# Down products of the experts with w2 stationary and rows moving, in halves of the rows, and the last expert done half by half

## The chip, the cores and the metric

The kernel runs on one core of a Trainium2 chip. The metric is the device time in microseconds (us) of one execution. The engines are named as the profile names them: PE (TensorE, the matmuls) with PEld (its weight loads), DVE (VectorE), ACT (ScalarE), POOL (GpSimd) and SP (SyncE, which issues most DMAs).

## The reference

A linear attention feeds a mixture of experts, which feeds a gated layer. What matters here is the middle part and the handing on to the last:

```python
for e in range(E):                       # 8 experts, x is 3072 x 384, F = 1024
    for k in range(2):                   # each token goes to its top 2 experts
        mask = top2[:, k] == e
        if not mask.any():
            continue
        h = np.maximum(x[mask] @ w1[e], 0.0)
        out[mask] += top2_w[mask, k, None] * (h @ w2[e])
...
a = x @ w_a                              # 384 x 1536 each
b = x @ w_b
return (a * b @ w_out).astype(np.float32)
```

## The kernel before

All is fp32, and every product is made of three matmuls on operands split in two (`prod3`: high by high, high by low, low by high; lines 799, 800 and 801 of the profile).

**Rows of an expert.** An expert gets about 768 of the tokens. Its rows are laid out for 832 (`CAP`); 768 of them (`MAIN`) are always computed, the last 64 only where the routing gave the expert more than 768. `more_rows[e]` is a register of PE, loaded from the tile `tails` (`load_more_rows`), and `tc.If` branches on it. In the profiled data experts 1, 2 and 7 have more than 768 rows and experts 0 and 3 to 6 have not: on line 835, in the other branch of `up_tail`, ten matmuls stand, two for each of five experts.

**Up phase** (`up_unit`). For each of 8 slices `f` of the hidden layer, w1 is stationary (128x128) and the rows X move, 384 columns at a time, twice: 9 matmuls for each, 144 for an expert. ACT writes the rectified high part H to `HB` (line 816), DVE the low part (line 817). Banks 2 to 5 of PSUM take turns.

**Tail and down phase.** `up_tail` does the last 64 rows the other way round (rows stationary, w1 moving, 18 matmuls of 512 columns), then 8 PE transposes bring them into `HB`. `down_unit(e, j)` takes 128 rows at a time: H is stationary and w2 moves (24 matmuls of 384 columns). ACT copies the bank out (`o`, line 890) and SP writes 128 rows to the DRAM tensor `y2` in one DMA (line 891). `down_tail` does the same for the last rows, or one filler matmul. Banks 6 and 7 take turns, so a unit can start when the unit two before it has been copied out.

**What runs beside it.** While expert e is computed, the rows of expert e+1 are gathered (POOL, line 478), transposed in blocks of 32 by DVE (`x_blocks`, line 506), written to the DRAM tensor `xt` and read back in pieces of 384 bytes (`x_out`, `x_in`: SP, lines 514 and 521), and split into X (`x_part`: ACT line 528, DVE line 529). That may not begin before X is free, so it stands in the down phase: `x_part(e+1, j)` goes ahead of `down_unit(e, j)` in the program. Weights come in chunks (`w_load` on SP, `w_split` on ACT and POOL), four chunks ahead. `bg` advances a decoding of the last layer's weights (DVE lines 953 to 963, POOL 960 and 961). Each engine works through its own instructions in the order in which the program wrote them.

**Handing on to the last layer.** For a block of 512 tokens `gather2` fetches both expert rows of each token from `y2` (POOL, line 986), `x2_sum` adds them, and the result is turned into the layout X2. For the first block this is done by PE transposes (`x2_unit`, line 486) inside the last unit of expert 7. The first block may only use the first 256 rows of expert 7 (`CAPL`, `early`), so `gather2` waits for the first two units of expert 7 alone. Later blocks go through DVE and `xt`, as the rows of the experts do. The last layer (`up2_unit`, `down2_unit`) starts when X2 is there; its chunks of weights lie in free parts of W, X, HB and in `EX` (7 slots).

Of the kernel before, what the change touches and what calls it, by code (L numbers as in the profile page):

```python
# [21 lines left out]
DM = H * D  # L22
# [9 lines left out]
CAPL = 256  # L32
CAP = 832
MAIN = 768
# [22 lines left out]
def moe_kernel(ctx: ExitStack, tc, qka, afirst, v, wgn, noise, w1, w2, w3, out):  # L57
# [736 lines left out]
    outs = sctx.enter_context(tc.tile_pool(name="outs", bufs=4))  # L794

    def prod3(ps, a, b, first, last):

        (ah, al), (bh, bl) = a, b
        nc.tensor.matmul(ps, ah, bh, start=first, stop=False)  # L799
        nc.tensor.matmul(ps, ah, bl, start=False, stop=False)  # L800
        nc.tensor.matmul(ps, al, bh, start=False, stop=last)  # L801

    upn = [0]

    def up_unit(e, f, cols):

        for s0, n in cols:
            s = slice(s0, s0 + n)
            pu = bank(2 + upn[0] % 4)[:, :n]
            upn[0] += 1  # L810
            for k in range(KD):
                ks = slice(k * 128, k * 128 + 128)
                prod3(pu, (w1h(f)[:, ks], w1l(f)[:, ks]), (Xh[:, k, s], Xl[:, k, s]), k == 0, k == KD - 1)
                if k == 1:
                    tick()
            nc.scalar.activation(Hh[:, f, s], pu, AF.Relu)  # L816
            nc.vector.scalar_tensor_tensor(Hl[:, f, s], pu, 0.0, Hh[:, f, s].bitcast(F32),  # L817
                                           op0=ALU.max, op1=ALU.subtract)
            tick()

    def up_tail(e):

        s = slice(CAP - 128, CAP)
        n = CAP - MAIN
        w = [W[:, i * 3072:i * 3072 + 3072].rearrange("p (f k n) -> p k f n", f=NF1, k=KD) for i in range(2)]
        pu = [bank(2 + (upn[0] + i) % 4) for i in range(2)]
        upn[0] += 2
        with tc.If(more_rows[e] > 0) as c:
            for i in range(2):
                f = slice(4 * i, 4 * i + 4)  # L830
                for k in range(KD):
                    prod3(pu[i], (Xh[:, k, s], Xl[:, k, s]), (w[0][:, k, f], w[1][:, k, f]), k == 0, k == KD - 1)
        with c.Else():
            for i in range(2):
                nc.tensor.matmul(pu[i], Xh[:, 0, s], w[0][:, 0, 4 * i:4 * i + 4], start=True, stop=True)
        hr = []
        if e < E - 1:
            t = tl(dec, [128, 2, 512], F32, "hr")
            for i in range(2):
                nc.scalar.activation(t[:, i], pu[i], AF.Relu)  # L840
                hr += [t[:, i, q * 128:q * 128 + 128] for q in range(4)]
        else:
            for q, m in ((0, 3), (3, 3), (6, 2)):
                t = tl(rows, [128, DM], F32, "row")
                for i in range(2):
                    a, b = max(q, 4 * i), min(q + m, 4 * i + 4)
                    if a < b:
                        nc.scalar.activation(t[:, (a - q) * 128:(b - q) * 128],
                                             pu[i][:, (a - 4 * i) * 128:(b - 4 * i) * 128], AF.Relu)
                hr += [t[:, c * 128:c * 128 + 128] for c in range(m)]  # L850
        yield
        pt = trbank()
        r = slice(128 - n, 128)
        with tc.If(more_rows[e] > 0) as c:
            for f in range(NF1):
                nc.tensor.transpose(pt[:, f * n:f * n + n], hr[f][r], ident[r, r])
        with c.Else():
            nc.tensor.matmul(pt[:, :NF1 * n], w2h(0)[:, :128], HB[:, :NF1 * n], start=True, stop=True)
        pt = pt[:, :NF1 * n].rearrange("p (f n) -> p f n", f=NF1)
        s = slice(MAIN, CAP)  # L860
        nc.scalar.activation(Hh[:, :, s], pt, AF.Copy)
        nc.vector.tensor_tensor(Hl[:, :, s], pt, Hh[:, :, s].bitcast(F32), op=ALU.subtract)
        yield

    def down_tail(e):
        s = slice(CAP - 128, CAP)
        pd = bank(6 + MAIN // 128 % 2)[:, :DM]
        with tc.If(more_rows[e] > 0) as c:
            for f in range(NF1):
                prod3(pd, (Hh[:, f, s], Hl[:, f, s]), (w2h(f), w2l(f)), f == 0, f == NF1 - 1)  # L870
        with c.Else():
            nc.tensor.matmul(pd, Hh[:, 0, s], w2h(0), start=True, stop=True)
        o = tl(outs, [128, DM], F32, "o")
        r0 = MAIN - (CAP - 128)
        nc.scalar.activation(o[r0:], pd[r0:], AF.Copy)
        nc.sync.dma_start(y2[base_of(e) + MAIN:base_of(e) + CAP], o[r0:])

    def down_unit(e, j, mid={}):
        c0 = min(128 * j, CAP - 128)
        s = slice(c0, c0 + 128)  # L880
        pd = bank(6 + j % 2)[:, :DM]
        for f in range(NF1):
            prod3(pd, (Hh[:, f, s], Hl[:, f, s]), (w2h(f), w2l(f)), f == 0, f == NF1 - 1)
            if f % 2:
                tick()
            if f in mid:
                mid[f]()
        o = tl(outs, [128, DM], F32, "o")
        r0 = 128 * j - c0
        nc.scalar.activation(o[r0:], pd[r0:], AF.Copy)  # L890
        nc.sync.dma_start(y2[base_of(e) + 128 * j:base_of(e) + c0 + 128], o[r0:])


    NEX = 7

    def w3_slot(n):
# [12 lines left out]
        c = 2 * KD * BLK + 6 * BLK + (n - 8) * 768  # L909
# [11 lines left out]
    def p_part(u):  # L921
        c = 2 * KD * BLK + 2 * BLK * (u % 3)
        return HB[:, c:c + BLK], HB[:, c + BLK:c + 2 * BLK]
# [93 lines left out]
    NA = CAPA // 128  # L1017
    for f in range(NF1):
        up_unit(0, f, [(0, CAPA)])
    small.clear()  # L1020
    for j in range(NA):
        down_unit(0, j, {f: (lambda q=q: x_unit(0, q)) for f, q in ((1, 3), (3, 4), (5, 5))} if j == NA - 1 else {})
    for f in range(NF1):
        if f == 1:
            x_unit(0, NJ - 1)
        up_unit(0, f, [(CAPA, MAIN - CAPA)])
        if f == 2:
            load_more_rows(0)
        if f >= NF1 - 4:
            w_load()  # L1030
        tick()
        bg()
# [4 lines left out]
    tail = up_tail(0)  # L1037
    next(tail)
    for n in range(3):
        down_unit(0, NA + n, {f: (lambda q=q: x_unit(1, q))  # L1040
                              for f, q in ((), ((0, 0), (3, 1), (6, 2)), ((0, 3), (2, 4), (4, 5), (6, 6)))[n]})
        next(tail, 0)
        for _ in range((3, 3, 2)[n]):
            w_split()
            w_load()
        bg()
    down_tail(0)

    for e in range(1, E - 1):
        for f in range(NF1):  # L1050
            up_unit(e, f, [(0, MAIN // 2), (MAIN // 2, MAIN // 2)])
            if f == 2:
# [14 lines left out]
        tail = up_tail(e)  # L1067
# [226 lines left out]
```

## Time and profile before

| | us |
|---|---|
| median of 3 executions (lowest, highest) | 1064.31 (1063.27, 1064.66) |
| the profiled execution | 1065.93 |
| its span, from the first to the last instruction | 1064.2 |
| PE busy in it | 1028.1 (97%) |
| DVE, ACT, POOL busy | 518.3, 417.9, 410.9 |
| mean granted TensorE clock, as a share of 2.4 GHz | 0.982 |

The span has three stages: attention with routing up to about 153 us, the experts up to about 608 us, the last layer to the end. The profile's matmul ends are modelled, and one matmul's record reaches into the next, so this document reads distances between the starts of matmuls, not their lengths. A row of the timeline has the start, the length, the engine, the line, the operation, output and inputs, and in brackets the idle time before it with what ended it.

### The profile page before, as it was taken

How to read it: one execution, taken by the hardware profiler on the slowest of the kernel's cores; microseconds unless marked ns; L12 is line 12 of the kernel's file. 1: busy time of each engine (PE TensorE's matmuls, PEld its weight loads, DVE VectorE, ACT ScalarE, POOL GpSimd, SP SyncE). 2: the span in 40 equal slices, each digit the busy share in tenths (PEclk: the TensorE clock that was granted, in tenths of full speed). 3: DMA queues.
4: the chain of work that ended last, by engine and by line, in shares of the span. 5: the costliest groups of instructions: out<-in, count | busy, mean ns of one | idle time of the engine just before them, and what ended most of it. 6: DMA issues, size and time to landing. Idle time of an engine off the chain costs nothing.

```text
span 1064.2 us, 17897 instructions
## 1 busy us (share of the span) xinstructions
PE 1028.1 (97%) x6868; PEld 950.8 (89%) x6868; DVE 518.3 (49%) x940; ACT 417.9 (39%) x913; POOL 410.9 (39%) x446
## 2 busy tenths in 40 slices
PE   8999689999999999999999899999999999999997
PEld 6988679999999999999999788888888888888886
DVE  7999666564554656575652445233242233332221
ACT  2455332564544555555554334322222222222212
POOL 4688432583755666666663443220020020000000
PEclk9999779999999999999999899999999999999999
DMA  7877111567575777686752534213022030020000
GB/s 275 289 284 270 53 54 51 183 211 203 178 214 173 214 226 217 202 241 211 236 171 80 186 89 126 90 45 75 30 76 44 30 109 11 30 60 1 30 1 32
DMA packets 98749, 141.04 MB, mean 133 GB/s; under 512 B 39520, under 2 KB 82656, under 8 KB 98656
## 3 DMA queue, kind: packets, MB, share of 16 engines
q1 hardware_dynamic: 92128, 120.13, 36.5%
q0 software_dynamic: 6528, 19.67, 6.0%
q8 instruction: 58, 0.95, 0.4%
q14 instruction: 35, 0.29, 0.1%
HBM read 101.43 MB, written 38.34 MB: 131 GB/s over the span
## 4 chain that ended last, share of the span: by engine, by line
PE 79%; DVE 6%; DMA 3%; POOL 2%; issue 2%; ACT 1%; SPq 0%; POOLq 0%; ACTq 0%; DVEq 0%
PE bank L799 25%; PE bank L800 25%; PE bank L801 25%; DMA raw<-xt 2%; DVE pm L655 1%; DMA xt<-tb 1%; DVE D L620 1%; DVE A L624 1%; PE bank L650 1%; PE bank L666 1%; PE bank L486 1%; SPq L521 0%; POOL row L986 0%; POOL row L478 0%; POOL W L110 0%
## 5 line engine op out<-in xcount | busy, mean ns | idle before, releaser
L110 POOL TENSOR_TENSOR W<-wst,W 128x384 fp32r<-128x384 f32 x136 | 140.3, 1037 | 138.7 <-ACT W L109 137.1
L799 PE MATMUL bank<-W,HB 128*128 128x384 f32 x528 | 179.9, 341 | 1.6 <-ACT o L890 1.6
L801 PE MATMUL bank<-W,HB 128*128 128x384 f32 x528 | 177.8, 337 | 0.0
L800 PE MATMUL bank<-W,HB 128*128 128x384 f32 x528 | 177.6, 336 | 0.0
L1127 DVE TENSOR_TENSOR p<-bank,a 128x512 f32<-128x512 f32 x72 | 49.8, 691 | 256.6 <-PE bank L801 252.4
L799 PE MATMUL bank<-X,W 128*128 128x384 f32 (+1 forms) x483 | 168.7, 349 | 0.8 <-DVE HB L817 0.8
L800 PE MATMUL bank<-X,W 128*128 128x384 f32 (+1 forms) x483 | 168.1, 348 | 0.0
L801 PE MATMUL bank<-X,W 128*128 128x384 f32 (+1 forms) x483 | 167.9, 348 | 0.0
L986 POOL DMA_INDIRECT row<-y,row x48 | 47.0, 979 | 187.7 <-DVE row L994 170.4
L1125 ACT ACTIVATE a<-bank 128x512 f32<-128x512 f32 x72 | 43.0, 597 | 165.6 <-PE bank L801 163.6
L1129 ACT ACTIVATE HB<-p 128x512 fp32r<-128x512 f32 x72 | 45.5, 632 | 157.3 <-DVE p L1127 150.4
L799 PEld LDWEIGHTS bank<-W,HB 128*128 128x128 f32 x528 | 100.0, 189 | 4.3 <-ACT o L890 2.6
L800 PEld LDWEIGHTS bank<-W,HB 128*128 128x128 f32 x528 | 99.9, 189 | 1.7
L801 PEld LDWEIGHTS bank<-W,HB 128*128 128x128 f32 x528 | 99.7, 189 | 0.0
L799 PEld LDWEIGHTS bank<-X,W 128*128 128x128 f32 x483 | 91.4, 189 | 5.0 <-DVE HB L817 1.3
L801 PEld LDWEIGHTS bank<-X,W 128*128 128x128 f32 x483 | 91.4, 189 | 3.9
L800 PEld LDWEIGHTS bank<-X,W 128*128 128x128 f32 x483 | 91.4, 189 | 3.9 <-issue 0.3
L817 DVE SCALAR_TENSOR_TENSOR HB<-bank,HB 128x384 fp32r<-128x384 f32 x128 | 68.7, 552 | 53.3 <-ACT HB L816 45.1
L816 ACT ACTIVATE HB<-bank 128x384 fp32r<-128x384 f32 x128 | 62.0, 490 | 81.1 <-PE bank L801 75.0
L478 POOL DMA_INDIRECT row<-xd,idx x56 | 59.4, 1061 | 40.0 <-DVE idx L387 23.1
L1130 DVE TENSOR_TENSOR HB<-p,HB 128x512 fp32r<-128x512 f32 x72 | 49.8, 692 | 50.2 <-ACT HB L1129 49.5
L109 ACT ACTIVATE W<-wst 128x384 fp32r<-128x384 f32 x144 | 73.0, 520 | 3.2 <-issue 2.1
(262 smaller groups left out, 1962.8 us busy)
## 6 DMA issues: line engine op xcount, KB each, us to landing
wst<-w SPq DMA_DIRECT2D x128, 192.0 KB
ring<-qka SPq DMA_DIRECT2D x22, 768.0 KB
wd<-w SPq DMA_DIRECT2D x36, 384.0 KB
y<-o SPq DMA_DIRECT2D x48, 192.0 KB
xt<-tb SPq DMA_DIRECT2D x11, 768.0 KB
raw<-xt SPq DMA_DIRECT2D x44, 192.0 KB
w3f<-u SPq DMA_DIRECT2D x36, 192.0 KB
wst<-w3f SPq DMA_DIRECT2D x36, 192.0 KB
```

Of the source, the lines that this page charges most:

```text
L109: nc.scalar.activation(h, raw, AF.Copy)
L110: eng.tensor_tensor(l, raw, h.bitcast(F32), op=ALU.subtract)
L478: nc.gpsimd.indirect_dma_start(out=t[:m], out_offset=None, in_=xd[:SPLIT * 128] if a else xd, in_offset=bass.IndirectOffsetOnAxis(ap=ix, a ...
L799: nc.tensor.matmul(ps, ah, bh, start=first, stop=False)
L800: nc.tensor.matmul(ps, ah, bl, start=False, stop=False)
L801: nc.tensor.matmul(ps, al, bh, start=False, stop=last)
L816: nc.scalar.activation(Hh[:, f, s], pu, AF.Relu)
L817: nc.vector.scalar_tensor_tensor(Hl[:, f, s], pu, 0.0, Hh[:, f, s].bitcast(F32), op0=ALU.max, op1=ALU.subtract)
L986: nc.gpsimd.indirect_dma_start(out=t, out_offset=None, in_=src, in_offset=bass.IndirectOffsetOnAxis(ap=row[:, i, k:k + 1], axis=0))
L1127: nc.vector.tensor_tensor(p, ps[1], a, op=ALU.mult)
L1129: nc.scalar.activation(h, p, AF.Copy)
L1130: nc.vector.tensor_tensor(l, p, h.bitcast(F32), op=ALU.subtract)
```

## The change

The down product is turned round: a 128x128 part of w2 is stationary and the rows of H move. The rows of an expert are cut into two halves in both phases: rows 0 to 415 and 416 to 831 (expert 0: 384 and 448). A product on the first half always has all its columns; one on the second half stands twice in the program, under `tc.If(more_rows[e] > 0)`: with 416 columns in one branch, and with 352 in the other (expert 0: 448 and 384). `up_tail` and `down_tail` are gone.

A down unit now gives 128 of the 384 outputs for a half of the rows, so there are six units: two halves `h` by three parts `k` (host code reorders w2 so that part k holds every third output). DVE takes the bank out with a transposition in blocks of 32 (`nc.vector.transpose`, line 874 of the changed kernel) in place of ACT's copy, and after the third part four DMAs write the half to `y2` in pieces of 384 bytes.

Expert 7 is done half by half: up and down of its first half, then up and down of its second. `CAPL` becomes 416, and the first block of the last layer is gathered and summed during the up phase of the second half; it now also goes through DVE and `xt` instead of PE transposes. The register is loaded ahead of the up phase. `EX` has 5 slots for 7, the ring of products in the last layer 2 for 3, the pool `outs` 2 larger buffers for 4.

```diff
-CAPL = 256
+CAPL = 416
+HALF = 416
...
+    def cols(e, h):
+        c = CAPA if e == 0 else HALF
+        return ((0, c), (c, CAP - c))[h]
+
+    def sized(e, h, emit):
+        n = cols(e, h)[1]
+        if h == 0:
+            return emit(n)
+        with tc.If(more_rows[e] > 0) as c:
+            emit(n)
+        with c.Else():
+            emit(n - (CAP - MAIN), n if e == 0 else 0)
...
-    def down_unit(e, j, mid={}):
-        c0 = min(128 * j, CAP - 128)
-        s = slice(c0, c0 + 128)
-        pd = bank(6 + j % 2)[:, :DM]
-        for f in range(NF1):
-            prod3(pd, (Hh[:, f, s], Hl[:, f, s]), (w2h(f), w2l(f)), f == 0, f == NF1 - 1)
...
-        nc.scalar.activation(o[r0:], pd[r0:], AF.Copy)
-        nc.sync.dma_start(y2[base_of(e) + 128 * j:base_of(e) + c0 + 128], o[r0:])
+    def down_unit(e, h, k, mid={}):
+        s0, n = cols(e, h)
+        pd = kept(6 + dnn[0] % 2)
...
+                prod3(pd, m, (w2h(f)[:, ks], w2l(f)[:, ks]), (Hh[:, f, s0:s0 + n], Hl[:, f, s0:s0 + n]),
+                      f == 0, f == NF1 - 1, first)
...
+        nc.vector.transpose(yt[:, :, :, k], pd[:, :n].rearrange("p (t r) -> p t r", r=32))
+        if k == KD - 1:
+            r0 = base_of(e) + s0
+            for c in range(4):
+                nc.sync.dma_start(y2[r0:r0 + n, 96 * c:96 * c + 96].rearrange("(t r) w -> r t w", r=32),
+                                  yts[0][32 * c:32 * c + 32, :n * KD].rearrange("r (t w) -> r t w", w=96))
...
     for f in range(NF1):
-        up_unit(e, f, [(0, MAIN // 2), (MAIN // 2, MAIN // 2)])
...
+        up_unit(e, f, 0)
         w_split()
         w_load()
...
+    for k in range(KD):
+        down_unit(e, 0, k)
         bg()
...
+    for f in range(NF1):
+        up_unit(e, f, 1)
+        if 2 <= f < 2 + TB:
+            gather2(f - 2)
+        if 4 <= f < 4 + TB:
+            x2_sum(f - 4)
+            x2_blocks(f - 4)
...
+    turn_out("x2", 0, BLK)
+    for k in range(KD):
+        if k == 0:
+            new_raw("x2")
+            turn_in(raws_of["x2"], 0, BLK)
...
+        if k == 2:
+            for i in range(TB):
+                x2_part(i)
+        down_unit(e, 1, k)
```

Where the instructions stand now is shown at three places.

PE, between the up and the down phase of expert 3, before: the branch of the tail, of which one side or the other is run, ahead of the first matmul on H (`HB`).

```order
L828 COMPARE_AND_BRANCH
...
L801 MATMUL bank_822_4773<-W_90,X_97 128x512
L828 UNCONDITIONAL_BRANCH
L835 MATMUL bank_821_4772<-W_90,X_97 128x512
L835 MATMUL bank_822_4773<-W_90,X_97 128x512
L828 UNCONDITIONAL_BRANCH
L799 MATMUL bank_825_4807<-W_90,HB_2392 128x384
```

PE, at the start of expert 3, in the changed kernel: the load of the register, a first half, and a second half in both branches.

```order
L1003 TENSOR_LOAD tails_85
...
L803 MATMUL bank_476_2399<-X_97,W_90 128x416
L824 COMPARE_AND_BRANCH
L801 MATMUL bank_481_2439<-X_97,W_90 128x416
...
L824 UNCONDITIONAL_BRANCH
L801 MATMUL bank_481_2439<-X_97,W_90 128x352
...
L824 UNCONDITIONAL_BRANCH
L801 MATMUL bank_486_2471<-X_97,W_90 128x416
```

The branches moved from three places of an expert to every product on a second half, 11 of them in an expert.

DVE, at the start of expert 3's down phase, before: the last block of rows for expert 4 (tb), then the parts of X, steps of the decoding (u, pw) between them, and nothing that reads a bank of the down phase.

```order
L506 STREAM_TRANSPOSE tb_4719<-row_4717 64x384
...
L529 TENSOR_TENSOR X_97<-raw_4754,X_97 128x3x128
L862 TENSOR_TENSOR HB_2392<-bank_827_4835,HB_2392 128x8x64
L529 TENSOR_TENSOR X_97<-raw_4754,X_97 128x3x128
L963 SCALAR_TENSOR_TENSOR u_4765<-wd_4691,rf_4768 128x384
L953 TENSOR_SCALAR u_4895<-wd_4800 128x384
L529 TENSOR_TENSOR X_97<-raw_4754,X_97 128x3x128
```

The same place in the changed kernel, where o is what is to be written to `y2`.

```order
L507 STREAM_TRANSPOSE tb_4974<-row_4972 64x384
L530 TENSOR_TENSOR X_97<-raw_5017,X_97 128x3x128
L874 STREAM_TRANSPOSE o_5068<-bank_503_2597 128x416
L530 TENSOR_TENSOR X_97<-raw_5017,X_97 128x3x128
L874 STREAM_TRANSPOSE o_5068<-bank_517_2650 128x416
L951 SCALAR_TENSOR_TENSOR u_5028<-wd_4938,rf_5031 128x384
L941 TENSOR_SCALAR u_5114<-wd_5037 128x384
L530 TENSOR_TENSOR X_97<-raw_5017,X_97 128x3x128
```

Taking out the banks (L874) has come into this queue; each one stands behind a part of X and, in some units, behind steps of the decoding.

DVE, at the end of expert 7, before: the sums of the first block's rows and their low parts out of PE's transposes.

```order
L994 SCALAR_TENSOR_TENSOR row_7445<-row_7445,wt_81,row_7443 128x384
L489 TENSOR_TENSOR X_97<-bank_1187_7542,X_97 128x3x128
L489 TENSOR_TENSOR X_97<-bank_1188_7554,X_97 128x3x128
```

The same in the changed kernel, from the last sum of the first block to the first product of the last layer (p).

```order
L982 SCALAR_TENSOR_TENSOR row_7851<-row_7851,wt_81,row_7849 128x384
...
L507 STREAM_TRANSPOSE tb_7822<-row_7851 128x384
...
L874 STREAM_TRANSPOSE o_7979<-bank_503_2597 128x416
...
L530 TENSOR_TENSOR X_97<-raw_7917,X_97 128x3x128 x4
L874 STREAM_TRANSPOSE o_7979<-bank_517_2650 128x416
L1119 TENSOR_TENSOR p_8143<-bank_942_8131,a_8141 128x512
```

Between the sum and X2 there are now a transposition on DVE, the way through `xt`, and four parts in a row.

## Rows read from the trace of the kernel before

**Rows 1.** The page, busy time, share of the span and instructions of each engine.

```profile
PE 1028.1 (97%) x6868; PEld 950.8 (89%) x6868; DVE 518.3 (49%) x940; ACT 417.9 (39%) x913; POOL 410.9 (39%) x446
```

**Rows 2.** Timeline of PE: first matmul of experts 1 to 7 and of the last layer.

```profile
215.54 0.34 PE L799 MATMUL bank<-X,W 128*128 128x384 f32 x1
...
274.62 0.33 PE L799 MATMUL bank<-X,W 128*128 128x384 f32 x1
...
333.69 0.33 PE L799 MATMUL bank<-X,W 128*128 128x384 f32 x1
...
385.27 0.33 PE L799 MATMUL bank<-X,W 128*128 128x384 f32 x1
...
436.89 0.33 PE L799 MATMUL bank<-X,W 128*128 128x384 f32 x1
...
489.74 0.33 PE L799 MATMUL bank<-X,W 128*128 128x384 f32 x1
...
540.55 0.33 PE L799 MATMUL bank<-X,W 128*128 128x384 f32 x1
...
608.51 0.39 PE L799 MATMUL bank<-X,EX 128*128 128x512 f32 x1
```

**Rows 3.** Timeline of PE: tail begins, down phase begins (expert 1); tail's filler (expert 3).

```profile
240.51 0.39 PE L799 MATMUL bank<-W,X 128*128 128x512 f32 x1
...
244.63 0.33 PE L799 MATMUL bank<-W,HB 128*128 128x384 f32 x1
...
358.65 0.63 PE L835 MATMUL bank<-W,X 128*128 128x512 f32 x2
```

**Rows 4.** Waits of PE, 150 to 600 us: us in total, times, longest.

```profile
PE bank L486 <- DVE X L489: 4.6, 1, 4.6
...
PE bank L799 <- ACT o L890: 1.6, 3, 0.6
```

**Rows 5.** Groups of DVE by form: busy us, mean ns of one, idle before.

```profile
L506 DVE STREAM_TRANSPOSE tb<-row 128x384 f32<-128x384 f32 x56 | 39.0, 696 | 4.9 <-DMA row<-xd,idx 4.1
```

**Rows 6.** Timeline of DVE: first part of X in the down phases of experts 1 to 6.

```profile
248.63 0.56 DVE L529 TENSOR_TENSOR X<-raw,X 128x384 fp32r<-128x384 f32 x1 [4.29 <-PE bank L799]
...
311.14 0.56 DVE L529 TENSOR_TENSOR X<-raw,X 128x384 fp32r<-128x384 f32 x1 [5.84 <-ACT X L528]
...
367.95 0.56 DVE L529 TENSOR_TENSOR X<-raw,X 128x384 fp32r<-128x384 f32 x1 [4.76 <-ACT X L528]
...
419.54 0.56 DVE L529 TENSOR_TENSOR X<-raw,X 128x384 fp32r<-128x384 f32 x1 [4.16 <-ACT X L528]
...
472.39 0.56 DVE L529 TENSOR_TENSOR X<-raw,X 128x384 fp32r<-128x384 f32 x1 [3.68 <-ACT X L528]
...
523.12 0.56 DVE L529 TENSOR_TENSOR X<-raw,X 128x384 fp32r<-128x384 f32 x1 [2.65 <-ACT X L528]
```

**Rows 7.** Timeline, expert 0: transposes of its last rows, and their low part.

```profile
187.55 0.55 PE L486 MATMUL bank<-ident,row 64*128 64x64 f32 x3
...
188.65 0.35 DVE L489 TENSOR_TENSOR X<-bank,X 128x192 fp32r<-128x192 f32 x1
```

**Rows 8.** Chain of waits at the end of expert 7: start, us, what.

```profile
579.66 2.52 DMA y<-o
...
583.03 0.33 POOL row L986
...
594.11 3.52 DMA row<-y,row
```

**Rows 9.** Timeline of SP, expert 1: rows of expert 2 go out to xt.

```profile
236.39 0.39 SPq L514 DMA_DIRECT2D xt<-tb  x1
```

**Rows 10.** A window: length, PE, PEld, DVE, ACT, POOL busy, granted clock, DMA share, GB/s.

```profile
600.00:604.00 4.00, 4.00 (x15) 3.90 (x16) 0.95 (x2) 1.00 (x3) 0.00 (x0) 0.50 0.00 0
```

**Rows 11.** The tail's branch on PE in expert 3, of the sequencer: ns, start.

```profile
L828 PEldq COMPARE_BRANCH  x1: 213/213/213, 355.5 to 355.5; - x1
```

**Rows 12.** Timeline of DVE, expert 3: a decoding step that waits for POOL.

```profile
372.70 1.35 DVE L963 SCALAR_TENSOR_TENSOR u<-wd,rf 128x384 int32<-128x384 int32 x1 [2.00 <-POOL rf L961]
```

More of the change, by code (lines that the diff above doesn't have):

```diff
@@ L793, in moe_kernel, with prod3 @@
     Hl = HB[:, NF1 * ROWS:].rearrange("p (f n) -> p f n", f=NF1)
-    outs = sctx.enter_context(tc.tile_pool(name="outs", bufs=4))
-    def prod3(ps, a, b, first, last):
+    outs = sctx.enter_context(tc.tile_pool(name="outs", bufs=2))
+    def prod3(ps, n, a, b, first, last, wide=0):
         (ah, al), (bh, bl) = a, b
-        nc.tensor.matmul(ps, ah, bh, start=first, stop=False)
-        nc.tensor.matmul(ps, ah, bl, start=False, stop=False)
-        nc.tensor.matmul(ps, al, bh, start=False, stop=last)
@@ L803, in moe_kernel, with kept @@
[L803 to L810, printed above, removed]
+        m = wide if first and wide else n
+        nc.tensor.matmul(ps[:, :m], ah, bh[:, :m], start=first, stop=False)
+        nc.tensor.matmul(ps[:, :n], ah, bl[:, :n], start=False, stop=False)
+        nc.tensor.matmul(ps[:, :n], al, bh[:, :n], start=False, stop=last)
+    upn, dnn = [0], [0]
+    held = {}
+    def kept(i):
+        if i not in held:
+            held[i] = bank(i)
+        return held[i]
@@ L811, in up_unit, with products @@
+    def cols(e, h):
[9 more added lines that the diff above has]
+            emit(n - (CAP - MAIN), n if e == 0 else 0)
+    def up_unit(e, f, h):
+        s0, n = cols(e, h)
+        pu = kept(2 + upn[0] % 4)
+        upn[0] += 1
+        def products(m, first=0):
             for k in range(KD):
@@ L819, in up_unit @@
-            tick()
[L821 to L854, printed above, removed]
-            for f in range(NF1):
[L856 to L863, printed above, removed]
@@ L878, in down_unit @@
-    def down_unit(e, j, mid={}):
-        c0 = min(128 * j, CAP - 128)
-        s = slice(c0, c0 + 128)
-        pd = bank(6 + j % 2)[:, :DM]
[L882 to L885, printed above, removed]
+        sized(e, h, products)
+        s = slice(s0, s0 + n)
+        nc.scalar.activation(Hh[:, f, s], pu[:, :n], AF.Relu)
+        nc.vector.scalar_tensor_tensor(Hl[:, f, s], pu[:, :n], 0.0, Hh[:, f, s].bitcast(F32),
+                                       op0=ALU.max, op1=ALU.subtract)
@@ new lines, in up_unit, with products @@
+        tick()
+    yts = {}
+    def down_unit(e, h, k, mid={}):
+        s0, n = cols(e, h)
+        pd = kept(6 + dnn[0] % 2)
+        dnn[0] += 1
+        ks = slice(k * 128, k * 128 + 128)
+        def products(f0, f1, m, first=0):
+            for f in range(f0, f1):
+                prod3(pd, m, (w2h(f)[:, ks], w2l(f)[:, ks]), (Hh[:, f, s0:s0 + n], Hl[:, f, s0:s0 + n]),
+                      f == 0, f == NF1 - 1, first)
+        f0 = 0
+        for f in sorted({*mid, NF1 - 1}):
+            sized(e, h, lambda m, first=0: products(f0, f + 1, m, first))
+            f0 = f + 1
+            tick()
@@ L1036, in moe_kernel @@
     tp = tc.alloc_tile_pool(name="tp", bufs=1, side="right")
[L1037 to L1043, printed above, removed]
+    for k in range(KD):
+        down_unit(0, 1, k, {f: (lambda q=q: x_unit(1, q))
+                            for f, q in (((6, 0),), ((1, 1), (4, 2), (6, 3)), ((1, 4), (3, 5), (5, 6)))[k]})
+        for _ in range((3, 3, 2)[k]):
             w_split()
@@ L1085, in moe_kernel @@
             bg()
+        bg()
     e = E - 1
+    load_more_rows(e)
     for f in range(NF1):
-        up_unit(e, f, [(0, MAIN // 2), (MAIN // 2, MAIN // 2)])
-        if f == 2:
-            load_more_rows(e)
+        up_unit(e, f, 0)
         w_split()
         w_load()
-        if f >= NF1 - 4:
-            load_more()
+        bg()
+    for k in range(KD):
+        down_unit(e, 0, k)
         bg()
```

106 lines of the change are left out of this document (43 added, 63 removed).

## The prediction

> **What bounds the kernel now.** I read the page's table of engines first: PE is busy for 1028.1 of the 1064.2 us of the span [rows 1], so a change gains only what it takes from PE's own time or from PE's few waits. Second comes the timeline of PE, at the first matmul of each expert [rows 2]. From one such start to the next, the experts take 59.08 (1), 59.07 (2), 51.58 (3), 51.62 (4), 52.85 (5) and 50.81 us (6); expert 7, up to the start of the last layer, takes 67.96. Experts 1, 2 and 7 run the tail, and pay some 7.5 us for it. Third, the waits of PE up to 600 us [rows 4]: 4.6 us once, before the last transposes of the hand-over to the last layer, and 1.6 us in all on the copies of the down banks. So the experts' stage is bound by PE, and the hand-over is the one place where PE stands.
>
> **What a product costs.** The distance between starts gives the price by width. Expert 3's up phase is 144 matmuls of 384 columns from 333.69 to its filler at 358.65 [rows 2, 3]: 0.1733 us each. Expert 1's tail is 18 matmuls of 512 columns from 240.51 to 244.63 [rows 3]: 0.2289 us each. The slope is 0.000434 us a column. It gives 0.1872 us for 416 columns, between two measured widths, and 0.1594 us for 352, which lies outside them. Its bounds are 0.1594 and 0.1733, since a narrower product may cost no less than one of 384; I take 0.1594, as the line holds between the two rows nearest to it.
>
> **Experts 1 to 6, matmuls alone.** After the change, an expert has 144 products in each half, 72 up and 72 down. With the tail that is 288 x 0.1872 = 53.91 us, without it 144 x (0.1872 + 0.1594) = 49.91 us.
>
> **The wait that the change adds.** A down bank is now emptied by DVE, with a transposition (T). Two banks take turns, so the third down unit waits for the first unit's T. On DVE that T stands behind the first part of X for the next expert, which needs rows that come back from `xt`. The subtraction of that part starts at 248.63, 311.14, 367.95, 419.54, 472.39 and 523.12 in experts 1 to 6 [rows 6]: 33.09, 36.52, 34.26, 34.27, 35.50 and 33.38 us after the first matmul. Add 0.56 for it, 0.70 for T (a block transposition of 128x384 takes 696 ns [rows 5]; from PSUM I bound it by 0.56 and 1.4) and 0.06 for the signal: the bank is free 1.32 us after that start. The chain to it runs beside the up phase, whose first six slices are slower by 6 x 18 x 0.0139 = 1.5 us in an expert with the tail (416 against 384 columns in both halves), so there I shift it by that. The third unit wants to start after 192 products: the 144 of the up phase and 48 of the first two units, both on the first half: 192 x 0.1872 = 35.94 us with extra rows, 72 x (0.1872 + 0.1594) + 48 x 0.1872 = 33.94 without.
>
> | expert | bank free | wanted | wait | after | before | gain |
> |---|---|---|---|---|---|---|
> | 1 | 35.91 | 35.94 | 0 | 53.91 | 59.08 | 5.17 |
> | 2 | 39.34 | 35.94 | 3.4 | 57.31 | 59.07 | 1.76 |
> | 3 | 35.58 | 33.94 | 1.6 | 51.51 | 51.58 | 0.07 |
> | 4 | 35.59 | 33.94 | 1.7 | 51.61 | 51.62 | 0.01 |
> | 5 | 36.82 | 33.94 | 2.9 | 52.81 | 52.85 | 0.04 |
> | 6 | 34.70 | 33.94 | 0.8 | 50.71 | 50.81 | 0.10 |
>
> Together 7.15 us gained. The waits come to 10.4 us; by my arithmetic they eat what the fillers and the tails of the experts without extra rows cost before.
>
> **Expert 0.** Its widths without extra rows stay at 384, so the phases cost the same. The fillers go: three products of 512 columns and one of 384, 3 x 0.2289 + 0.1733 = 0.86 us. Its last rows are transposed right ahead of the second half, which needs them: from 187.55 to the end of the low part at 188.65 + 0.35 takes 1.45 us [rows 7], of which the transposes ran before too; I take 1.0 us of wait (0.8 to 1.2). Eleven first products run 64 columns wider than needed, 11 x 64 x 0.000434 = 0.3 us. Expert 0 loses 0.4 us.
>
> **Expert 7.** Let T7 be the end of the down products of its first half: 144 x 0.1872 = 26.96 us. From there the hand-over is a chain. The last matmul's drain and T, 1.0 us (estimate, from the 0.70 above). The write of `y2`: 2.52 us in one DMA [rows 8]; now four DMAs write pieces of 384 bytes, for which I take 4.0, between 2.52 and 6.1 (half of the way through `xt` below, which also moves pieces of 384 bytes, out and in). Then 0.85 us until the gather starts (582.18 to 583.03 [rows 8]), 11.08 us of gathers (583.03 to 594.11), 3.52 for the last to land [rows 8], 0.56 for the sum, 0.70 for its block transposition, 12.24 us through `xt` (236.39, the issue, to 248.63, the first subtraction [rows 6, 9]), and four parts of X2, 4 x 0.56 = 2.24. Sum 36.2 us, so the last layer starts 26.96 + 36.2 = 63.15 us after expert 7. PE is out of work at 53.91, so it stands for some 9 us. In the trace of before, after a wait of 4.6 us [rows 4], the granted clock was 0.50, the lower of the two levels (1.2 GHz), from 600 to 604 us [rows 10]: 4 us at half speed, 2.0 us lost. I add them again: 65.2 against 67.96, a gain of 2.8 us.
>
> **What costs nothing.** A branch takes 213 ns of PE's sequencer, which reaches it at 355.5, 3.1 us before its matmul at 358.65 [rows 3, 11]: the queue of waiting products covers it, and the load of the register. Without that cover each of the 95 branches would cost its 0.2 us, 20 us in all. ACT loses seven copies in an expert; it is busy for 39% [rows 1], so that gains nothing. DVE gets six T, 4.2 us, at 49%: nothing but the wait above. SP issues eight writes instead of seven; weights are read four chunks ahead.
>
> **Sum.** 7.15 - 0.4 + 2.8 = 9.55 us. The profiled execution took 1065.93 us, 1.62 above the median of 1064.31; taken from it, 1056.4, and from the median **1054.8 us**. About 0.2%, 2.1 us, is what a measurement of this kernel tells from no change.
>
> **The rivals.**
> - *DVE's queue holds PE at every unit* (slower). In the down phase T also stands behind steps of the decoding, one of which waits 2.00 us for POOL and then runs 1.35 [rows 12]. Between one unit's T and the next there are 24 x 0.1872 = 4.49 us, filled with 0.56 + 0.70. If those 3.35 us are exposed in full once in each of six experts, 20.1 us are lost: 1074.9. It turns slower than before from (9.55 + 2.1) / 6 = 1.9 us an expert on. For it: T is the only reader of the banks, and cannot pass the decoding. Against: 3.2 us of every 4.49 are slack. Chance 0.10.
> - *No wait at the third unit* (faster). The first part of X came late partly because it was queued behind the tail and the copies on ACT, which go. If nothing waits, the 10.4 us are gained: 1044.4. Against: in five of the six experts the subtraction waits for ACT's part of the same rows [rows 6], the end of a chain through `xt` that the change leaves as it is. Chance 0.14.
> - *A product of 352 columns costs what one of 384 does.* Four experts x 144 x 0.0139 = 8.0 us less: 1062.8. No row shows a narrower one at rate. Chance 0.08.
> - *Branches cost more than the sequencer's lead.* It has 18 products, about 3.1 us, from one branch to the next in the up phase. If taking one costs 0.3 us more than that, on the 62 of experts without extra rows, PE loses 62 x 0.3 = 19 us: about 1073. Against: before, one branch an expert left the lead intact. Chance 0.04.
> - *The hand-over is later.* If the writes of 384-byte pieces take 8.0 us for 4.0, expert 7 gains nothing: 1058.8. Chance 0.12.
>
> On the fourth, the Trainium skill ("Runtime: NRT & Kernel Launch", section Instruction fetch mechanics) says that a taken branch whose target lies outside the two pages of instructions at hand waits for a fetch by DMA, and calls this a reason to unroll rather than branch. Here a branch skips one or two dozen instructions, so that by this rule few would leave the pages; the rows show 213 ns for one and cannot show 95.
>
> On the fifth, the Trainium skill ("DMA: Bandwidth & Descriptors", section Specifications) names 512 bytes as the least for full rate, with a read-modify-write below that. The change turns writes of whole rows into pieces of 384 bytes, against this rule; by it the case of 8.0 us would be the likelier one, and the sum 1058.8. No row of before shows the time of such a write alone.
>
> **How the numbers follow.** The forecast with its small errors has 0.52, the rivals 0.48. The range reaches from 1046, near the case without waits, to 1063, which holds the late hand-over and the 352 columns without gain; beyond it lie most of the two slow rivals and part of the fast one, some 0.2. Faster: the forecast, the second and fifth rivals and half of the third, 0.80 to 0.82, taken as 0.80; the same: 0.07, from the third and the milder cases of the first; slower: 0.13, the first and the fourth.
>
> **What would show it.** Starts of matmuls 0.187 us apart at 416 columns and 0.159 at 352; one wait of PE an expert in the down phase, on DVE's L874, 0 to 3.4 us as in the table, 10 us in all; expert lengths as in its column "after"; in expert 7 a chain of y2, gathers, `xt`, with PE idle for some 9 us and the lower clock behind it. It would be wrong if PE waits on `o` in every unit, if the gaps at branches exceed 0.2 us, or if the last layer starts more than 68 us after expert 7.

## The result and the profile after

The changed kernel took 1071.07 us (median of 7 runs, 1067.55 to 1071.62) against 1063.27 us for the kernel before (7 runs of this comparison, 1062.18 to 1064.66): a ratio of 1.0066, with an interval of 1.0052 to 1.0080. The change made it slower by some 7 us. The prediction was 1054.8 us, with a range of 1046 to 1063: wrong in sign and in size.

The page gives the first hint: PE has 16 us less to do than before [rows 1], and the span is 4.5 us longer.

```profile
PE 1012.1 (95%) x6686; PEld 932.8 (87%) x6686; DVE 555.3 (52%) x984; ACT 384.8 (36%) x831; POOL 416.6 (39%) x446
```

The timeline of PE, at the first products of the experts and of some phases, answers to [rows 2].

```profile
212.63 0.35 PE L801 MATMUL bank<-X,W 128*128 128x416 f32 x1
...
239.89 0.35 PE L801 MATMUL bank<-HB,W 128*128 128x416 f32 x1
...
267.07 0.35 PE L801 MATMUL bank<-X,W 128*128 128x416 f32 x1
...
323.88 0.35 PE L801 MATMUL bank<-X,W 128*128 128x416 f32 x1
...
376.42 0.35 PE L801 MATMUL bank<-X,W 128*128 128x416 f32 x1
...
429.41 0.35 PE L801 MATMUL bank<-X,W 128*128 128x416 f32 x1
...
454.85 0.35 PE L801 MATMUL bank<-HB,W 128*128 128x416 f32 x1
...
482.83 0.35 PE L801 MATMUL bank<-X,W 128*128 128x416 f32 x1
...
535.77 0.35 PE L801 MATMUL bank<-X,W 128*128 128x416 f32 x1
...
556.17 0.35 PE L801 MATMUL bank<-HB,W 128*128 128x416 f32 x1
...
569.73 0.35 PE L801 MATMUL bank<-X,W 128*128 128x416 f32 x1
...
609.01 0.80 PE L801 MATMUL bank<-X,EX 128*128 128x512 f32 x1 [4.05 <-ACT X L529]
```

The distances between these starts, by stage, beside those of before and what the prediction made of them (the last stage runs to the end of the span):

| stage | before | after | change | forecast |
|---|---|---|---|---|
| expert 0 | 62.42 | 62.97 | +0.55 | +0.4 |
| expert 1 | 59.08 | 54.44 | -4.64 | -5.17 |
| expert 2 | 59.07 | 56.81 | -2.26 | -1.76 |
| experts 3 to 6 | 206.86 | 211.89 | +5.03 | -0.22 |
| expert 7 | 67.96 | 73.24 | +5.28 | -2.8 |
| last layer | 455.69 | 459.69 | +4.00 | 0 |
| sum | 911.08 | 919.04 | +7.96 | -9.55 |

The sum, 7.96 us, is what the medians differ by (7.8). The spans differ by less, since in the first profile of before the first expert starts 3.46 us later than in this one (153.12 against 149.66); a second profile of before, below, shows that this is not the change.

The waits of PE from 150 to 625 us answer to [rows 4], where two rows held 6.2 us.

```profile
PE bank L801 <- DVE o L874: 8.2, 5, 2.1
PE bank L801 <- DVE HB L846: 6.2, 3, 4.3
PE bank L801 <- ACT X L529: 4.1, 1, 4.1
PE bank L802 <- DVE HB L846: 3.5, 2, 2.6
```

The first row is the wait that was forecast, at the third down unit. The second and the fourth are waits for H, which nobody forecast, and the largest of them, 4.3 us, stands in expert 7's first up half: 556.17 - 535.77 = 20.40 us where 72 products without a wait take 13.6.

### The profile page after: what moved, and what is told of

The parts are those of the page before. It is cut to its first block, busy times and chain, and to the rows that moved or that the text cites. A ratio compares the mean times of both kernels' runs of the same rounds, so it can differ in the third digit from the quotient of the medians.

```text
span 1068.7 us, 17559 instructions
## 1 busy us (share of the span) xinstructions
PE 1012.1 (95%) x6686; PEld 932.8 (87%) x6686; DVE 555.3 (52%) x984; ACT 384.8 (36%) x831; POOL 416.6 (39%) x446
## 4 chain that ended last, share of the span: by engine, by line
PE 70%; DVE 8%; DMA 8%; issue 2%; SPq 2%; POOL 2%; ACT 1%; POOLq 0%; ACTq 0%; DVEq 0%
PE bank L801 22%; PE bank L802 22%; PE bank L803 22%; DMA xt<-tb 3%; DMA wd<-w 2%; DMA raw<-xt 2%; SPq L522 1%; DVE pm L656 1%; DVE D L621 1%; DVE A L625 1%; DMA wst<-w3f 1%; DVE HB L846 1%; PE bank L667 1%; PE bank L651 1%; SPq L878 1%
## 5 line engine op out<-in xcount | busy, mean ns | idle before, releaser
L111 POOL TENSOR_TENSOR W<-wst,W 128x384 fp32r<-128x384 f32 x136 | 145.7, 1082 | 121.2 <-ACT W L110 113.6
L801 PE MATMUL bank<-HB,W 128*128 128x416 f32 (+4 forms) x474 | 168.9, 356 | 8.8 <-DVE o L874 8.2
L801 PE MATMUL bank<-X,W 128*128 128x416 f32 (+4 forms) x474 | 169.8, 358 | 6.6 <-DVE HB L846 6.2
L802 PE MATMUL bank<-HB,W 128*128 128x416 f32 (+3 forms) x474 | 168.1, 355 | 3.7 <-DVE HB L846 3.5
L802 PE MATMUL bank<-X,W 128*128 128x416 f32 (+3 forms) x474 | 168.6, 356 | 0.0
L803 PE MATMUL bank<-X,W 128*128 128x416 f32 (+3 forms) x474 | 168.4, 355 | 0.0
L803 PE MATMUL bank<-HB,W 128*128 128x416 f32 (+3 forms) x474 | 167.7, 354 | 0.0
L801 PEld LDWEIGHTS bank<-HB,W 128*128 128x128 f32 x474 | 89.8, 189 | 14.8 <-DVE o L874 10.3
L845 ACT ACTIVATE HB<-bank 128x416 fp32r<-128x416 f32 (+2 forms) x128 | 65.1, 516 | 102.9 <-PE bank L803 94.5
L846 DVE SCALAR_TENSOR_TENSOR HB<-bank,HB 128x416 fp32r<-128x416 f32 (+2 forms) x128 | 73.2, 585 | 54.4 <-ACT HB L845 52.1
L801 PEld LDWEIGHTS bank<-X,W 128*128 128x128 f32 x474 | 90.3, 191 | 11.7 <-DVE HB L846 7.5
L802 PEld LDWEIGHTS bank<-HB,W 128*128 128x128 f32 x474 | 89.8, 189 | 8.4 <-DVE HB L846 4.1
L803 PEld LDWEIGHTS bank<-X,W 128*128 128x128 f32 x474 | 90.2, 190 | 4.2
L802 PEld LDWEIGHTS bank<-X,W 128*128 128x128 f32 x474 | 90.3, 191 | 3.7
L803 PEld LDWEIGHTS bank<-HB,W 128*128 128x128 f32 x474 | 89.7, 189 | 4.0
```

The lines of the kernel that those rows point to most:

```text
L111: eng.tensor_tensor(l, raw, h.bitcast(F32), op=ALU.subtract)
L801: nc.tensor.matmul(ps[:, :m], ah, bh[:, :m], start=first, stop=False)
L802: nc.tensor.matmul(ps[:, :n], ah, bl[:, :n], start=False, stop=False)
L803: nc.tensor.matmul(ps[:, :n], al, bh[:, :n], start=False, stop=last)
L845: nc.scalar.activation(Hh[:, f, s], pu[:, :n], AF.Relu)
L846: nc.vector.scalar_tensor_tensor(Hl[:, f, s], pu[:, :n], 0.0, Hh[:, f, s].bitcast(F32), op0=ALU.max, op1=ALU.subtract)
```

## Experiments

Five parts of the change are disputed: the price of the widths, the branches, the place of T on DVE, what holds H in expert 7, and the hand-over. The first four kernels each touch one. Gains against the change are differences of medians from separate comparisons. By the ratios to the kernel before, `t_first`, `y2_late`, `hand_pe` and all three repairs gain 6.3, 6.7, 7.8 and 27.4 us, each give or take some 2 us.

**Halves of 384** (`halves_384`). Edit:

```diff
-CAPL = 416
+CAPL = 384
-HALF = 416
+HALF = 384
```

> Edit: the halves of experts 1 to 7 are 384 and 448 or 384 rows by branch, as expert 0 has them, in place of 416 and 416 or 352. Theory W (the price of a product does not follow my line: in the changed kernel 416 columns stand 0.1885 us apart and 352 stand 0.1655): two products of 384 cost 2 x 0.1733 against 0.354, so an expert without extra rows loses 144 x 0.0074 = 1.1 us, four of them 4.3 us; those with extra rows about 0.4 us each; in all some 5 us, to about 1066. Rival (w2 stationary and rows moving makes every product dearer, whatever its width): 384 columns also stand more than 0.176 us apart, and the gain is below 2 us.

Measured: 1077.21 us, ratio 1.0125 (1.0108 to 1.0141): 6 us slower than the change, where both theories had it faster or level. Theory W was right on the price: where nothing waits, an up phase without extra rows took 24.96 us (experts 5 and 6), 0.1733 a product, against 25.44. But the waits of PE on o grew from 8.2 to 13.4 us:

```profile
PE bank L801 <- DVE o L874: 13.4, 6, 3.1
```

In expert 2 the third unit starts 38.5 us after the expert's first product in both kernels (the bank is free then, not earlier), so what the products save is waited. And the longer wait is paid twice. The windows behind it, of halves_384 and then of the change (columns as in [rows 10]):

```profile
308.00:312.00 4.00, 4.00 (x16) 4.00 (x15) 2.76 (x4) 3.10 (x7) 3.62 (x4) 0.57 0.71 173
```

```profile
308.00:312.00 4.00, 4.00 (x23) 3.96 (x22) 2.64 (x4) 2.71 (x7) 3.92 (x5) 1.00 0.38 102
```

After a gap of 3.00 us between products the granted clock was 0.57 and PE started 16 matmuls in 4 us; after one of 2.42 us, in the change, it stayed at 1.00 with 23. Most of the loss is in expert 4, 58.3 us for 53.0: there both a wait for H (2.0 us for 1.3) and the one on o (2.7 for 0.7) were longer, and the clock fell behind each, to 0.68 and to 0.59.

**No branch** (`no_branch`). Edit: `sized` always emits all columns.

```diff
-        if h == 0:
-            return emit(n)
+        return emit(n)
```

> Edit: no branch; the second half has always all its 416 columns (448 in expert 0), also where the expert has no extra rows. Theory (branches cost nothing, a product of 352 columns saves 0.1885 - 0.1655 us): experts 3 to 6 get 144 x 0.023 = 3.3 us longer, expert 0 some 144 x 0.023 = 3.3 us, in all 13 to 17 us, to about 1086; experts 1 and 2 keep 54.4 and 56.8 us. Rival (branches hold PE): experts 1 and 2 get shorter by over 1 us, and the whole gets less than 8 us longer.

Measured: 1082.41 us, ratio 1.0182 (1.0161 to 1.0204), 11.3 us slower than the change. Experts 3 to 6 got 2.1, 2.1, 2.8 and 1.6 us longer, expert 0 2.9, expert 1 stayed (54.51 us against 54.44). Expert 2 did not stay as expected: it took 58.25 us for 56.81, with a gap of 2.63 us at its third unit and a granted clock of 0.61 behind it. Neither got shorter without its branches, so branches cost nothing that shows; a narrow second half is worth what its columns save, less the part that a wait on o takes back (those waits fell from 8.2 to 3.7 us here).

**T ahead of the first part of X** (`t_first`). Edit, in the loop over the down units:

```diff
-            x_part(e + 1, i)
+            if i:
+                x_part(e + 1, i)
...
             down_unit(e, h, k)
+            if i == 0:
+                x_part(e + 1, 0)
```

> Edit: the first part of X for the next expert stands behind the first down unit in the program, so that on DVE the transposition that empties the first bank no longer stands behind it. Theory (the wait at the third unit is this queue): the waits on o in experts 2 to 6, 9 us in all, go, and nothing takes their place: about 1062. Rival: the wait moves to the fourth unit or to the start of the next expert, where X is late: gain below 4 us.

Measured: 1064.9 us, ratio 1.0007 (0.9992 to 1.0023), 6.2 us faster than the change. DVE around the first T of expert 2, in the change:

```profile
304.30 0.56 DVE L530 TENSOR_TENSOR X<-raw,X 128x384 fp32r<-128x384 f32 x1 [3.85 <-ACT X L529]
304.78 0.74 DVE L874 STREAM_TRANSPOSE o<-bank 128x416 f32<-128x416 f32 x1
```

and in t_first, where T runs 3.4 us ahead of the same subtraction:

```profile
303.43 0.69 DVE L874 STREAM_TRANSPOSE o<-bank 128x416 f32<-128x416 f32 x1
306.87 0.56 DVE L530 TENSOR_TENSOR X<-raw,X 128x384 fp32r<-128x384 f32 x1 [2.75 <-ACT X L529]
```

The waits on o fell from 8.2 to 1.4 us, and experts 2, 3, 5 and 6 got 1.2 to 2.3 us shorter. So this wait was DVE's queue, as the theory said. Expert 4 gave 2 us back: its up phase took 30.07 us for 27.02, with a gap of 3.14 us that is not on o. That one belongs to the next question.

**Decoding done before expert 7** (`decode_early`). Edit: one more `bg()` behind the fourth slice's first half, in experts 1 to 6.

> Edit: one more step of the decoding in each of experts 1 to 6, so that none is left in expert 7. Theory (in the first half of expert 7, which is done at twice the pace of a whole slice, ACT stands at a decoding step whose transfer has not landed, and H behind it): the first up half of expert 7 falls from 20.4 to about 13.7 us, and the hand-over with it: about 1064.5. Rival (weights at twice the pace, or the splits, are what it waits for): it stays above 18 us, and the time within 2 us of the change's.

Measured: 1071.36 us, ratio 1.0079 (1.0050 to 1.0108): no gain. Yet the place named was right: expert 7's first up half took 13.56 us for 20.40, without a gap. But experts 1 to 6 together got 8.2 us longer, mostly experts 1, 3 and 4: the waits on o grew from 8.2 to 12.1 us, and a gap on H in expert 4 from 1.64 to 3.16. A step less in one place is a step more in another, so the question became why a decoding step holds ACT at all.

**What makes it late.** The start of expert 4 in the change, first SP:

```profile
373.98 0.33 SPq L952 DMA_DIRECT2D w3f<-u  x1
377.40 1.96 SPq L878 DMA_DIRECT2D y<-o  x4
379.46 1.13 SPq L115 DMA_DIRECT2D wst<-w  x2
380.65 0.44 SPq L933 DMA_DIRECT2D wd<-w  x1
```

then ACT:

```profile
380.17 0.52 ACT L110 ACTIVATE W<-wst 128x384 fp32r<-128x384 f32 x1
385.33 0.56 ACT L939 ACTIVATE ah<-wd 128x384 f32<-128x384 f32 x1 [4.65 <-DMA wd<-w]
385.79 0.53 ACT L940 ACTIVATE rf<-wd 128x384 f32<-128x384 uint32 x1
386.23 0.91 ACT L845 ACTIVATE HB<-bank 128x416 fp32r<-128x416 f32 x2
```

SP issues nothing for 3.1 us, until the last T of expert 3 is done, and takes 2.0 us for the four writes; the load of wd stands behind them, and ACT can go on 4.7 us after its issue. ACT meets the step that needs it at 380.7 and stands until 385.33, with H (L845) behind it, and PE runs out of free banks (the next product starts at 387.41). From expert 1 to 7, ACT's waits for wd were 6.3 us in 7 before and are 48.8 in 15 now; before the change, the change:

```profile
ACT ah L951 <- DMA wd<-w: 6.3, 7, 2.1
```

```profile
ACT ah L939 <- DMA wd<-w: 48.8, 15, 6.8
```

In expert 7 the same wait of ACT is 6.40 us long, and PE's gap behind it the largest. This was tried with the writes alone moved.

**Writes to y2 later** (`y2_late`). Edit (`flush` runs what `late` holds, behind the next down unit and behind the second slice of the next expert, the third in expert 7):

```diff
-            for c in range(4):
-                nc.sync.dma_start(y2[...], yts[0][...])
+            def write(o=yts[0]):
+                for c in range(4):
+                    nc.sync.dma_start(y2[...], o[...])
+            if e == E - 1:
+                write()
+            else:
+                late.append(write)
```

> Edit: the four writes of a half to y2 stand later in the program (first halves behind the next down unit, second halves behind the second slice of the next expert); those of expert 7 stay where they are. Theory S (on SP the four writes wait for the third transposition, and loads of weights for the decoding, wd, stand behind them; ACT then stands at the decoding step that needs wd, H behind it, and PE behind H): ACT's waits for wd, 48.8 us from expert 1 to 7 in the changed kernel and 6.3 before, fall below 20 us; the first up half of expert 7 falls from 20.4 to about 14 us and expert 4's up phase from 27.0 to 25.5: about 1063. Rival (wd is late because the DMA engines are busy, or because the pace is higher): ACT's waits stay above 35 us, and the time within 2 us of the change's.

Measured: 1062.49 us, ratio 1.0003 (0.9992 to 1.0015), 8.6 us faster than the change, with 6.0 of it in expert 7. Its first up half took 13.56 us, expert 4's up phase 25.44. SP's waits for T ahead of the writes, in the change and in y2_late:

```profile
SPq L878 <- DVE o L874: 67.1, 13, 15.7
```

```profile
SPq L885 <- DVE o L880: 21.5, 4, 15.6
```

ACT's waits for wd fell to 24.8 us: halved, though not below the 20 expected. What makes the other half was not tried. SP at the start of expert 7 now loads wd at 533.85, ahead of the writes and 1.3 us ahead of the expert's first product; in the change it did so at 541.39, behind them and 5.6 us after that product. And ACT waits 0.25 us there for 6.40:

```profile
533.85 0.42 SPq L944 DMA_DIRECT2D wd<-w  x1
...
541.81 2.06 SPq L885 DMA_DIRECT2D y<-o  x4
```

```profile
538.21 0.56 ACT L950 ACTIVATE ah<-wd 128x384 f32<-128x384 f32 x1 [0.25 <-DMA wd<-w]
```

The rival asked for waits above 35 us and the time of the change, and got neither. The pace is the same in both kernels. The writes' traffic did move in time, but the load itself took nearly as long: from its issue until ACT went on, 5.3 us in the change (541.39 to 546.66) and 4.4 in y2_late (533.85 to 538.21). Its issue came 6.9 us earlier, measured from the expert's first product.

**Sums later** (`sum_late`). Edit: `x2_sum` and `x2_blocks` of the first block stand behind the up units of expert 7's second half.

> Edit: the sums of the first block's rows and their transpositions on DVE stand behind the whole up phase of expert 7's second half, not inside it. Theory (in the changed kernel they wait on DVE and ACT for gathered rows, with the last slices' H behind them, so that PE stands some 5 us between 586 and 593 us; but the last layer waits for a chain through gathers and xt that does not pass PE): those waits go, the wait ahead of the last layer grows by as much, and the time stays within 2 us of the change's. Rival (each wait of PE counts): 5 us less and 2 to 3 us of low clock less, about 1063.

Measured: 1070.12 us, ratio 1.0061 (1.0040 to 1.0082), within 1 us of the change. The gaps at 586 to 593 us went from five to one of 3.72 us, which is on o, and PE's wait ahead of the last layer grew from 4.1 to 8.2 us. PE's waits for H there were covered by the later one, as the theory said.

**PE transposes in the hand-over** (`hand_pe`). Edit, besides that of sum_late:

```diff
-        if k == 2:
-            for i in range(TB):
-                x2_part(i)
-        down_unit(e, 1, k)
+        down_unit(e, 1, k, {f: (lambda q=q: x2_unit(q)) for f, q in
+                            (((1, 0), (3, 1), (5, 2), (7, 3)) if k == 2 else ())})
```

and no `turn_out`, `turn_in` for this block.

> Edit: as sum_late, and the first block of the last layer is turned by PE transposes inside the last down unit, as in the kernel before, in place of DVE and xt. Theory (the way through xt, 14 us from its issue to the first subtraction, is the end of the chain, and the low clock behind the wait costs 2 to 4 us more): the last layer starts some 9 us earlier, about 64 us after expert 7, at the full clock: about 1059. Rival (the gathers alone are late): the transposes wait as long, and the gain is below 4 us.

Measured: 1061.38 us, ratio 0.9993 (0.9973 to 1.0013), 9.7 us faster than the change. Expert 7 took 66.1 us for 73.2 (64 were expected) and the last layer 454.1 for 459.7, so that a good part of the gain came behind the hand-over, where the clock no longer fell. In the change, the chain of waits ahead of the last layer reads:

```profile
594.37 3.74 DMA xt<-tb
...
602.56 6.00 DMA wst<-w3f
608.58 1.96 DVE X L530 x4
```

From the issue to the first subtraction it takes 14.2 us, and the link ahead of the subtraction is not `xt` but a chunk of weights for the last layer: the four parts of X2 stand behind splits (L111) in DVE's queue.

**All three** (`combo`). Edit: t_first, y2_late and hand_pe together.

> Edit: the three repairs together (first part of X behind the first down unit; the writes to y2 later; sums later and PE transposes for the first block). Theory (three separate new waits): the gains add up, 6 us of the bank waits, some 8 of the writes and 12 of the hand-over, to about 1045, below the kernel before. Rival (one late thing hides behind another): above 1058.

Measured: 1042.21 us, ratio 0.9808 (0.9792 to 0.9824), 28.9 us less than the change and 2% less than the kernel before. The single gains, 6.2, 8.6 and 9.7, add up to 24.5 (by the ratios 20.8 for 27.4); together they give more, among other things because expert 4's gap in t_first went too (50.46 us for 55.04). Experts 1 to 6 took 54.49, 54.82, 51.00, 50.46, 51.05 and 50.91 us, near the 53.91 and 49.91 of matmuls alone.

**Sums behind the first unit** (`combo2`). Edit: in combo, the sums go behind `down_unit(7, 1, 0)`.

> Edit: as combo, with the sums of the first block behind the first down unit of expert 7's second half, so that this unit's transposition does not stand behind them on DVE. Theory: combo's wait of 3.05 us at the third unit (574.35 us), and the low clock behind it, go: some 4 us less than combo's 1042.2, about 1038. Rival (the PE transposes wait for the rows instead): less than 1 us gained.

Measured: 1042.55 us, ratio 0.9813 (0.9788 to 0.9839): no gain. The gap at the third unit went (its products stand 0.19 us apart from the start), and the transposes of the rows inside that unit wait instead:

```profile
PE bank L487 <- DVE X L490: 3.6, 1, 3.6
```

The rival had it right: behind one late thing stood another.

**Combo2 with halves of 384** (`combo2_384`).

> Edit: combo2 with halves of 384 and 448 or 384 rows, the edit of halves_384. Theory (halves_384 lost because PE, faster between the waits, only waited longer, and the longer waits drew the low clock; with the waits gone the price of the products decides): experts 3 to 6 gain 1.0 us each (0.1733 twice against 0.1885 and 0.1655, as rows of the runs show), experts 1 and 2 lose 0.2: some 3.5 us less than combo2. Rival (unequal halves or the wider transposition cost by themselves): slower than combo2 by 2 us or more.

Measured: 1042.11 us, ratio 0.9801 (0.9778 to 0.9824): neither theory. Up phases without extra rows took 24.96 us, but the waits on o came back, 5.1 us for combo2's 1.1, with 2.59 us at the fourth unit of expert 5, whose bank is freed by a T that still stands behind a part of X. Only expert 7 got clearly shorter, 57.5 us for 62.0, and the last layer gave 2.3 us of that back.

**The kernel before once more.**

> No edit: the kernel before once more, for a second profile. Theory: the 3 us by which the first expert starts earlier in the profile of the changed kernel (150.15 against 153.12 us) lie in the first 45 us, which the change does not touch, and vary from execution to execution: here the first expert starts at 150 to 153 us, and the lengths of the experts are those of the first profile within 0.5 us. Rival (the change moves something there): 153 us again.

Measured: a span of 1061.1 us, with the first expert's first product at 149.79 us (the 150.15 named in the expectation is the second product of the change; its first is at 149.66). From there to the end it took 911.3 us, 911.08 in the first profile; experts 1 to 6 took 59.08, 59.07, 51.63, 51.29, 53.04 and 50.81 us. So the 3.46 us at the start vary by execution.

## Why the prediction was wrong

**Experts 1 and 2: right.** -4.64 and -2.26 us against -5.17 and -1.76. The wait at the third unit was 0 in expert 1, and in expert 2 the gap of 2.42 us less a spacing, 2.2, for 3.4. In experts 3 to 6 it was 1.8, 0.9, 2.3 and 1.8 for 1.6, 1.7, 2.9 and 0.8; in all 9.0 for 10.4 (by the starts; the idle time of the waits is the 8.2 above). The mechanism was the predicted one, and t_first shows it.

**The price of the widths: a little low.** Expert 1's up phase is 144 products of 416 columns in 27.26 us, 0.1893 each for 0.1872. Expert 5's is 72 of each width in 25.44; there 352 columns stand 0.165 us apart, between the bounds of 0.1594 and 0.1733. That is 0.5 us an up phase. In down phases the 352 columns stood 0.158 us apart in expert 3 and 0.167 in expert 5; why they differ was not tried. With these prices and the waits, two thirds of the 5.25 us by which experts 3 to 6 missed are explained; most of the rest is expert 4's gap of 1.45 us, from SP.

**SP's queue: the step that failed.** "SP issues eight writes instead of seven; weights are read four chunks ahead" counted issues, and put what waits behind them at nothing. In the kernel before, a write waits for one unit's copy; now four in a row wait for the third T, with loads of wd behind them, which the program issues two steps of the decoding, and not four chunks, ahead of their use. SP did not wait longer for the units in all. Before, the row reads

```profile
SPq L891 <- ACT o L890: 99.8, 34, 12.7
```

against the 67.1 us in 13 waits shown above. A single wait got longer, 5.2 us for 2.9 on average, and everything behind it comes later at once. The result is a wait of ACT, then of H, then of PE, two engines away from the queue that the change touched. One of the prediction's signs of being wrong came: the last layer started 73.24 us after expert 7, more than 68. In expert 7 the wait made T7 33.96 us for the 26.96 of the forecast: 7.0 us, of which 4.5 are the gap, and most of the rest is the low clock behind it (0.50 from 548 to 552 us). The delay also feeds itself. ACT had waited as long for the load of wd before that; this held a part of X, and the last T of expert 6 stood behind that part:

```profile
535.23 0.56 ACT L939 ACTIVATE ah<-wd 128x384 f32<-128x384 f32 x1 [6.82 <-DMA wd<-w]
```

```profile
536.67 0.83 DVE L530 TENSOR_TENSOR X<-raw,X 128x384 fp32r<-128x384 f32 x2 [1.07 <-ACT X L529]
537.42 0.74 DVE L874 STREAM_TRANSPOSE o<-bank 128x416 f32<-128x416 f32 x1
```

So T came 1.7 us after expert 7's first product (0.2 in y2_late), and the writes and the next load of wd with it. Expert 7's pace, a step of the decoding in every 1.7 us, is no cause by itself: y2_late has the same pace and no gap in that half. This step is the largest of several: with the writes moved, the kernel was still 7.7 us above the forecast, for the reasons above and below.

**The chain of the hand-over: 3.1 us too short, and with other links.** From T7 to the last layer it took 39.3 us, against 36.2. The links differ: the first gather started 9.0 us behind T7 for 5.85, since it stands on POOL behind a split that waited for weights (until 577.56), and the way to X2 took 14.2 us for 12.24. What the four writes took is not shown in the change, where the gather that needs them waited for POOL anyway. In y2_late, where expert 7's writes stand as in the change, their issues and landings are:

```profile
L885 SPq DMA_DIRECT2D y<-o x4: 319/490/516, 563.2 to 564.7; - x4
...
DMA to landing us min/median/max: 2.1/3.4/4.4
```

So they took at most 5.9 us, where the sum had 4.0 with bounds of 2.52 and 6.1. There too POOL was held until later: its first gather was issued at 571.26.

**The clock behind the wait: too little.** I took 2.0 us from one window behind the 4.6 us wait of before [rows 10]. The window after it is slow too, so by the two clocks that wait cost some 2.8 us (an estimate: half of 4 us and a fifth of 4):

```profile
604.00:608.00 4.00, 4.00 (x21) 4.00 (x20) 2.18 (x3) 1.60 (x4) 1.01 (x1) 0.80 0.62 188
```

In the change the windows at the start of the last layer read:

```profile
608.00:612.00 4.00, 2.21 (x4) 1.45 (x5) 3.18 (x6) 0.96 (x3) 0.24 (x1) 0.53 0.34 102
612.00:616.00 4.00, 4.00 (x13) 3.11 (x12) 0.00 (x0) 0.60 (x1) 0.00 (x0) 0.61 0.93 233
```

The first 36 products took 11.76 us (609.01 to 620.77) where they took 8.20 before: 3.56 us, of which 0.8 are a wait for a part of X2 and most of the rest the clock. Expert 7 and the last layer missed by 12.1 us together: 7.0 from T7, 3.1 from the chain, and 2.0 here, since the last layer lost 4.0 where the forecast had put 2.0 into expert 7.

**The rivals.** The first rival had the sign and the kind, an engine's queue that holds PE once more, but the wrong queue: the only waits on o in experts 1 to 6 are the five at the third unit, and those stand behind X, not behind the decoding. Branches are out: in the up phase of expert 5 the largest distance from a product of 352 columns to the next slice was 0.17 us. The Trainium skill ("Runtime: NRT & Kernel Launch", section Instruction fetch mechanics) warns of a fetch when a taken branch leaves the pages at hand; no run here shows one at these branches, with 0.32 us, once, as the largest such distance in expert 3. (A branch of the down phase skips 48 instructions, 24 matmuls with their weight loads, and not the one or two dozen of the prediction.) The fifth rival, 8.0 us for the writes of 384-byte pieces, did not come: the 5.9 us above are below it, and what held the first gather was POOL. The writes hurt by their place in SP's queue.

## What to carry to other kernels

When a change makes DMAs wait for a new producer, list what is queued behind them on the same engine and how much reserve each of these has: here writes that nobody was in a hurry for cost 8.6 us (6.7 by the ratios) by delaying the loads behind them. Ask it of every queue that a new instruction joins, and put what is not urgent behind what is. And before narrowing the work between two waits, see whether the wait is pinned to something else: halves of 384 made the products cheaper and the kernel slower.

## What was not expected of the hardware

A stall of PE costs more than its length, and how much cannot be read from its length alone. After a wait of 2.2 us at a third unit in the change (a gap of 2.42) the granted clock stayed at 1.00, while in y2_late a gap of 2.16 us was followed by 0.66 and 0.91:

```profile
516.00:520.00 4.00, 3.04 (x10) 2.90 (x11) 2.67 (x5) 3.87 (x10) 3.78 (x4) 0.66 0.43 126
520.00:524.00 4.00, 4.00 (x22) 3.95 (x21) 3.94 (x5) 0.00 (x0) 2.87 (x3) 0.91 0.96 254
```

In that expert (6) it lengthened the down phase to 29.18 us, 1.7 more than in the change, where the gap was 2.00 us. What decides between the two was not tried.
